# First keys loaded through GpSimd's own queue, and the second unit of a sketch-attention kernel divided by token

## The chip, the cores and the metric

The kernel runs on one core of one Trainium2 chip. A core has TensorE (matrix products, PE in the profile, with its weight loads as PEld), VectorE (DVE), ScalarE (ACT), GpSimd (POOL) and SyncE (SP), which here only issues transfers, and 16 DMA engines that all queues share. SBUF is the memory on the core; PSUM receives what TensorE computes. The metric is the time of one execution on the device in microseconds (us).

## What is computed

Two parts follow each other. The first is an attention in which the softmax is replaced by a product of two sketches, so that keys can be summed up first; the second is a mix of four experts with ReLU, weighted by gates.

```python
# q, k, v: (4 batches, 4 heads, 1088 tokens, 32); S1, S2: (8, 32)
def phi(x):
    a = np.einsum('rd,bhsd->bhsr', S1, x)
    b = np.einsum('rd,bhsd->bhsr', S2, x)
    return np.einsum('bhsi,bhsj->bhsij', a, b).reshape(*x.shape[:-1], r * r)   # 64 features
q_p, k_p = (phi(q), phi(k))
kv = np.einsum('bhsf,bhsd->bhfd', k_p, v)
z = np.sum(k_p, axis=2)
num = np.einsum('bhsf,bhfd->bhsd', q_p, kv)
den = np.einsum('bhsf,bhf->bhs', q_p, z)[..., None] + 1e-06
attn = num / den
x = attn.transpose(0, 2, 1, 3).reshape(4352, 128)
# experts: w1 (4, 128, 1024), w2 (4, 1024, 128), gates (4352, 4)
p = domain_probs / (domain_probs.sum(-1, keepdims=True) + 1e-09)
for e in range(4):
    h = np.maximum(x @ w1[e], 0.0)
    out += p[:, e:e + 1] * (h @ w2[e])
```

All of it is in float32. No query of a batch can be worked on before all keys of that batch are projected, multiplied and summed.

## The kernel before

The 4352 tokens are worked on in chunks by the experts (128, 448, 512 tokens and so on) and in units by the attention (128, 448 and 512 for the first batch). The attention leaves its result in `xT`, 128 partitions (4 heads x 32) by 4352 tokens, from which the experts' first products read. While the experts of one chunk run, the attention of later units is done in small pieces between their steps: each `yield` below ends a piece, and a rate that is reckoned from `needed` says how many pieces a step takes in.

The first loads, all on the sync queue but one half of S:

```python
    def load_rows(src, b, name, part=slice(0, S)):
        d = kn if name == "kn" else qn
        if b not in d:
            d[b] = lpool.tile([P, S], F32, tag=name, bufs=2, name=name)
        c, n = part.start, part.stop - part.start
        nc.sync.dma_start(d[b][:, part], bass.AP(src.tensor, src.offset + b * H * S * D + c, [[G * D, P], [1, n]]))
    ...
    for i, (eng, src) in enumerate(((nc.scalar, S1), (nc.sync, S2))):
        eng.dma_start(s_raw[R * i : R * i + R, :], src.bitcast(I32))
    ...
    load_rows(k, 0, "kn")                    # 128 rows of 1088 float32
    load_rows(q, 0, "qn", slice(0, P))       # 128 rows of 128 float32
    vn[0] = load_v(0)                        # four transfers of 128 KB, two of 16 KB
    warm = cpool.tile([P, 512], BF16, name="warm")
    nc.vector.memset(warm[:, :], 0.0)
    ...
    nc.sync.dma_start(dp..., domain_probs...)      # the gates' load
    ...                                            # ends, the rest of q, and the weights
    nc.gpsimd.memset(sk[:, :], 0.0)                # GpSimd's first instruction here
    ...                                            # memsets of sr, sq, kT, vx, own2, eps on GpSimd
    def keep_warm(n):
        for _ in range(n):
            wp = psum(ps_h, "h")
            nc.tensor.matmul(wp[:, :], warm[:, 0:P], warm[:, :], start=True, stop=True)

    keep_warm(10)
```

`keep_warm` multiplies zeros. VectorE then turns S1 and S2 into float32 (`s_T`), and ScalarE and GpSimd copy this into the block matrices `sk` (keys) and `sr` (first queries). What follows for the first batch and unit:

```python
    def start():
        for r in range(3):
            key_turn(b, r)                    # VectorE: kn -> kT
        qT = query_turn(b, 0, n)              # VectorE: qn -> qT
        ...
        key_project(b, 0, kf[0])              # TensorE: h <- sk, kT; ScalarE: fs
        key_project(b, 1, kf[1])
        next(value)                           # ScalarE: vn -> vx
        key_project(b, 2, kf[2])
        ...                                   # TensorE: o, num <- qT, sr
        ...                                   # VectorE and GpSimd: kp, the products of features
        ...                                   # TensorE: f <- vx, kp, the sum over the keys
        ...                                   # VectorE: qp, then kvz
        first = attend_first(b, 0, n, qp)
        ...
        key_blocks(b, kv)                     # VectorE: kvx
```

The division of the first two units goes by feature: numerator and denominator come with the tokens along the free axis, and the result goes straight into `xT`.

```python
    def attend_first(b, c, n, qp):
        nd = [psum(ps_n, "den"), psum(ps_n, "num")]
        ...                                   # for c == 0: 1e-6 added by a product with eps
        for i in range(2):
            for _ in range(2):
                on_side(lambda s: nd[i][half[s], 0:n], lambda s: kvzs[b][:, s, 1 - i, :],
                        lambda s: qp[s][:, 0:n], start=(i > 0 or c > 0), stop=True)
        yield
        nc.vector.transpose(dT[:, 0:n], nd[0][:, 0:n])
        yield
        ...                                   # for c > 0: add 1e-6
        nc.vector.reciprocal(rc[:, 0 : n // 32], column)
        nc.vector.transpose(_ap(rb, ...), _ap(rc, ...))       # spread over the 32 values of a head
        yield
        nc.vector.tensor_tensor(out=_ap(xT, 0, P, c, order), in0=nd[1]..., in1=rb..., op=ALU.mult)
        have[0] += n
        yield
```

All later units go by token: a tile of 128 tokens lies on the partitions, four heads of 32 numerators and one denominator along the free axis, and the quotient has to be turned back, through memory outside the core.

```python
    def attend(b, c, n, qp):
        nd = [psum(ps_n, "den"), psum(ps_n, "num")]
        for c0, m in unit_parts(b, c, n):
            T = blocks(m)                     # tiles on each side; (4, 3) for 448 tokens, (4, 4) for 512
            for t in range(T[0]):
                for p in range(2):
                    for _ in range(2):
                        ...
                        on_side(lambda s: nd[i][half[s], ...], lambda s: qp[p][:, at : at + HP],
                                lambda s: kvx[b][:, p, :], start=True, stop=True)   # 66 columns
        yield
        ...                                   # rc = 1 / (den + 1e-6), small
        yield
        ...                                   # xs = num * rc
        yield
        nc.vector.transpose(_ap(y, ...), _ap(xs, ...))
        ...                                   # sync: y -> xd (4 transfers), xd -> xT (1 transfer)
        have[0] += n
        yield

    def queries(b, c, n):
        ...                                   # qT, qc, qf, qb, qa, qp
        yield from (attend_first if b == 0 and c < START[2] else attend)(b, c, n, qp)
```

At step 13 of the first chunk GpSimd copies one column of `xT` (`behind`) and so waits for the second unit, before it starts its sums of weight blocks (`w2s`), which TensorE reads from the second chunk on.

Of the kernel before, what the change touches and what calls it, by code (L numbers as in the profile page):

```python
# [8 lines left out]
F32 = mybir.dt.float32  # L9
BF16 = mybir.dt.bfloat16  # L10
I32 = mybir.dt.int32
ALU = mybir.AluOpType
# [11 lines left out]
def kernel(  # L24
# [23 lines left out]
    nc = tc.nc  # L48

    P = 128  # L50
    HP = 64
    B, H, S, D = q.shape
# [31 lines left out]
        return pool.tile([P, 512], F32, tag=tag, name=tag)  # L84


    def load_rows(src, b, name, part=slice(0, S)):

        d = kn if name == "kn" else qn
        if b not in d:  # L90
            d[b] = lpool.tile([P, S], F32, tag=name, bufs=2, name=name)
        c, n = part.start, part.stop - part.start
        nc.sync.dma_start(d[b][:, part], bass.AP(src.tensor, src.offset + b * H * S * D + c, [[G * D, P], [1, n]]))

    def load_v(b):
        t = lpool.tile([P, H * NT * D], F32, tag="vn", name="vn")
# [15 lines left out]
    def load_batch(b):  # L112
        load_rows(k, b, "kn")
        vn[b] = load_v(b)
        load_rows(q, b, "qn")

    s_raw = cpool.tile([R2, 2 * D], I32, name="s_raw")
    for i, (eng, src) in enumerate(((nc.scalar, S1), (nc.sync, S2))):
        eng.dma_start(s_raw[R * i : R * i + R, :], src.bitcast(I32))  # L119
# [6 lines left out]
    def load_w2(e):  # L126
        nc.sync.dma_start(w2_sb[:, e], w2[e].rearrange("(f p) d -> p f d", p=P))

    load_rows(k, 0, "kn")
    load_rows(q, 0, "qn", slice(0, P))  # L130
    vn[0] = load_v(0)


    warm = cpool.tile([P, 512], BF16, name="warm")
# [5 lines left out]
    nc.sync.dma_start(  # L140
        dp.rearrange("p g e -> p (g e)"), bass.AP(domain_probs.tensor, domain_probs.offset, [[G * E, P], [1, G * E]])
    )

    ends = cpool.tile([P, 2, E], F32, name="ends")
    e_sum = cpool.tile([P, 2, 3], F32, name="e_sum")
# [31 lines left out]
    def keep_warm(n):  # L177

        for _ in range(n):
            wp = psum(ps_h, "h")  # L180
            nc.tensor.matmul(wp[:, :], warm[:, 0:P], warm[:, :], start=True, stop=True)  # L181

    keep_warm(10)


    turn = [0]
# [271 lines left out]
    def query_turn(b, c, n):  # L458


        qT = apool.tile([P, QW], F32, tag="qT", name="qT")
        for c0, m in unit_parts(b, c, n):
            src = c + c0
            if b == 0 and c < START[2]:
                todo = [([[1, m]], [[1, m]], 0, 0)]
            elif c0:
                todo = [([[32, 4], [1, 32]], [[1, 4], [4, 32]], 0, 0)]
            else:
                T = blocks(m)
                if T[0] == T[1]:  # L470
                    todo = [([[32 * T[0], 4], [32, T[0]], [1, 32]], [[32, 4], [P, T[0]], [1, 32]], 0, 0)]
                else:
                    todo = [
                        ([[32 * T[s], 2], [32, T[s]], [1, 32]], [[32, 2], [P, T[s]], [1, 32]], 64 * T[0] * s, HP * s)
                        for s in range(2)
                    ]
            for i, o, ci, co in todo:
                nc.vector.transpose(_ap(qT, 0, P, c0 + co, o), _ap(qn[b], 0, P, src + ci, i))
        return qT
# [12 lines left out]
    def attend_first(b, c, n, qp):  # L492


        nd = [psum(ps_n, "den"), psum(ps_n, "num")]
        if c == 0:
            for _ in range(2):
                on_side(
                    lambda s: nd[0][half[s], 0:n],
                    lambda s: _ap(vx, 0, P, D, [[0, HP]]),  # L500
                    lambda s: _ap(eps, 0, P, 0, [[0, n]]),
                    start=True,
                    stop=False,
                )
        for i in range(2):
            for _ in range(2):
                on_side(
                    lambda s: nd[i][half[s], 0:n],
                    lambda s: kvzs[b][:, s, 1 - i, :],
                    lambda s: qp[s][:, 0:n],  # L510
                    start=(i > 0 or c > 0),
                    stop=True,
                )
        yield
        dT = apool.tile([P, UNITS[0][1]], F32, tag="dT", name="dT")
        nc.vector.transpose(dT[:, 0:n], nd[0][:, 0:n])
        yield
        rc = apool.tile([P, QW // 32], F32, tag="rc", name="rc")
        column = _ap(dT, 0, P, 0, [[32, n // 32]])
        if c:  # L520
            nc.vector.tensor_scalar(
                out=rc[:, 0 : n // 32], in0=column, scalar1=1e-6, scalar2=1.0, op0=ALU.add, op1=ALU.mult
            )
            column = rc[:, 0 : n // 32]
        nc.vector.reciprocal(rc[:, 0 : n // 32], column)
        rb = apool.tile([P, UNITS[0][1]], F32, tag="rb", name="rb")
        nc.vector.transpose(
            _ap(rb, 0, P, 0, [[32, n // 32], [1, 32]]), _ap(rc, 0, P, 0, [[1, n // 32], [0, 32]])
        )
        yield  # L530

        order = [[1, 4], [4, 32]] if c == 0 else [[32, n // 32], [1, 32]]
        nc.vector.tensor_tensor(  # L533
            out=_ap(xT, 0, P, c, order),
            in0=nd[1][:, 0:n].rearrange("p (g j) -> p g j", j=32),
            in1=rb[:, 0:n].rearrange("p (g j) -> p g j", j=32),
            op=ALU.mult,
        )
        have[0] += n
        yield  # L540

    def attend(b, c, n, qp):

        nd = [psum(ps_n, "den"), psum(ps_n, "num")]
        W = H * (D + 1)
        tiles = 0
        laid = []
        for c0, m in unit_parts(b, c, n):  # L550
            T = blocks(m)
# [4 lines that stand above are left out]
                        at = c0 + P * t + (HP * turn[0] if t < T[turn[0]] else 0)  # L556
                        i, k = divmod(tiles + t, 3)
                        on_side(
                            lambda s: nd[i][half[s], W * k + W // 2 * p : W * k + W // 2 * (p + 1)],
                            lambda s: qp[p][:, at : at + HP],  # L560
                            lambda s: kvx[b][:, p, :],
                            start=True,
                            stop=True,
                        )
            laid.append((c0, T, tiles))
            tiles += T[0]
        yield
        banks = [(i, 3 * i, min(tiles, 3 * i + 3)) for i in range((tiles + 2) // 3)]
        rc = apool.tile([P, QW // 32], F32, tag="rc", name="rc")
        for i, t0, t1 in banks:  # L570
            nc.vector.tensor_scalar(
                out=rc[:, H * t0 : H * t1],
                in0=_ap(nd[i], 0, P, D, [[D + 1, H * (t1 - t0)]]),
                scalar1=1e-6, scalar2=1.0, op0=ALU.add, op1=ALU.mult,
            )
        nc.vector.reciprocal(rc[:, 0 : H * tiles], rc[:, 0 : H * tiles])
        yield
        xs = apool.tile([P, QW], F32, tag="qa", name="xs")
        for i, t0, t1 in banks:
            nc.vector.tensor_tensor(  # L580
                out=_ap(xs, 0, P, P * t0, [[D, H * (t1 - t0)], [1, D]]),
                in0=_ap(nd[i], 0, P, 0, [[D + 1, H * (t1 - t0)], [1, D]]),
                in1=_ap(rc, 0, P, H * t0, [[1, H * (t1 - t0)], [0, D]]),
                op=ALU.mult,
            )
        yield
        y = apool.tile([P, QW], F32, tag="y", name="y")
        for c0, T, t0 in laid:
            nc.vector.transpose(
                _ap(y, 0, P, P * t0, [[32, T[0]], [32 * T[0], H], [1, 32]]),  # L590
                _ap(xs, 0, P, P * t0, [[P, T[0]], [D, H], [1, D]]),
            )
            m = 64 * sum(T)
            base = xd.offset + P * (S * b + c + c0)
            for a in range(4):
                run = 32 * T[a // 2]
                nc.sync.dma_start(
                    bass.AP(
                        xd.tensor,
                        base + a // 2 * 64 * T[0] + a % 2 * run,  # L600
                        [[m, 32], [32 * m, H], [1, run]],
                    ),
                    _ap(y, 32 * a, 32, P * t0, [[32 * T[0], H], [1, run]]),
                )
            nc.sync.dma_start(
                xT[:, S * b + c + c0 : S * b + c + c0 + m],
                bass.AP(xd.tensor, base, [[m, P], [1, m]]),
# [5 lines that stand above are left out]
# [22 lines left out]
                yield  # L635
        yield
        yield
        yield from (attend_first if b == 0 and c < START[2] else attend)(b, c, n, qp)


    w2s = cpool.tile([P, E, FB // 2, 4, HP], F32, name="w2s")
# [277 lines left out]
    for b in range(B):  # L919
        count += 17 if b else 0  # L920
        for n in UNITS[b] if b else UNITS[0][1:]:
            count, columns = count + 19, columns + n
            for m in range(NC):
                if columns - n < START[m] + CHUNKS[m] <= columns:
                    needed[m] = count
# [70 lines left out]
```

## Time and profile before

| What | Value |
|---|---|
| median of three times | 490.6 us (490.52 to 491.0) |
| span of the profiled run | 488.9 us |
| TensorE busy | 482.5 us (99%) |
| VectorE, ScalarE, GpSimd busy | 322.1, 244.7, 226.6 us |
| share of TensorE in the chain that ended last | 96% |
| clock granted to TensorE | 1.00 throughout |
| memory traffic | 26.24 MB, mean 54 GB/s |

How to read it. Each line of the timeline is one instruction, or a run of like ones: its start and duration in us, the engine, the line in the kernel, the operation, what it writes and reads (destination <- source), the shape, and in brackets the idle time of its engine before it with what ended that. TensorE's float32 products show as two passes each, so 16 products are counted as 32. "SPq" is the issue of a transfer by the sync engine; the landing comes later. The chain of waits starts at the last instruction and is followed back: at each step to what released it, or to the instruction before it on its engine. A helper records most matrix products, so they all have its line; the tile names tell them apart: `h` holds key projections first and expert products later, `f` the key sums, `den` and `num` the second unit's products.

### The profile page before, as it was taken

Reading aid. Unit: us, or ns where it says so; the run is one execution under the profiler, and the core shown is the slowest. Engines: PE = TensorE matmul, PEld = TensorE weight load, DVE = VectorE, ACT = ScalarE, POOL = GpSimd, SP = SyncE. Lnnn points to the kernel's source line nnn. Section 1 sums busy time; section 2 is a strip of 40 time slices with the busy share of each in tenths; the row PEclk is TensorE's granted clock in tenths of the full one; section 3 lists DMA queues with packets and bytes.
Section 4 is the critical chain, followed back from the end, with each engine's and each line's share of the span. In section 5 each row is a group of like instructions: output and inputs, shape, how many; then the busy total and the mean of one; then the engine's idle time right before and its main releaser. Section 6 shows DMA issues by size and latency. Waiting matters only on the chain.

```text
span 488.9 us, 11239 instructions
## 1 busy us (share of the span) xinstructions
PE 482.5 (99%) x4498; PEld 358.8 (73%) x4498; DVE 322.1 (66%) x752; ACT 244.7 (50%) x488; POOL 226.6 (46%) x261
## 2 busy tenths in 40 slices
PE   8999999999999999999999999999999999999997
PEld 5877777677777777555777777777777777878996
DVE  5759685868676757768675665575575566655642
ACT  4344563455445634535455464445455455566651
POOL 6051473516345444334555353434555345555570
PEclk9999999999999999999999999999999999999999
DMA  7990230040102420041102200021101200120000
GB/s 209 289 297 10 87 96 1 11 127 1 34 1 87 117 71 1 0 119 24 34 1 87 50 0 3 0 87 24 33 1 56 50 0 1 50 50 2 16 1 18
DMA packets 37587, 26.24 MB, mean 54 GB/s; under 512 B 26016, under 2 KB 34592, under 8 KB 37024
## 3 DMA queue, kind: packets, MB, share of 16 engines
q1 hardware_dynamic: 37520, 25.53, 18.8%
q8 instruction: 35, 0.57, 0.5%
q14 instruction: 16, 0.13, 0.1%
q10 hardware_dynamic: 16, 0.00, 0.0%
HBM read 21.28 MB, written 4.24 MB: 52 GB/s over the span
## 4 chain that ended last, share of the span: by engine, by line
PE 96%; DVE 2%; DMA 1%; issue 0%; ACT 0%; SPq 0%; DVEq 0%
PE h L193 49%; PE o L193 40%; PE f L193 4%; PE den L193 2%; DMA kn<-in_k_dram 1%; DVE qp L485 1%; DVE hid L745 1%; PE num L193 0%; PE h L181 0%; DVE kT L319 0%; ACT hid L770 0%; DVE qa L631 0%; ACT sh L889 0%; SPq L119 0%; DVE xT L533 0%
## 5 line engine op out<-in xcount | busy, mean ns | idle before, releaser
L193 PE MATMUL h<-xT,w_sb 128*64 128x512 f32 (+4 forms) x1408 | 300.0, 495 | 0.3 <-DVE xT L533 0.3
L745 DVE SCALAR_TENSOR_TENSOR hid<-h,hid 128x256 f32<-128x256 f32 (+6 forms) x432 | 203.8, 472 | 143.4 <-ACT hid L770 134.6
L770 ACT ACTIVATE hid<-h 128x512 f32<-128x512 f32 (+3 forms) x288 | 158.3, 550 | 195.2 <-PE h L193 151.4
L193 PE MATMUL o<-hid,w2s 128*64 128x256 f32 (+3 forms) x1152 | 221.9, 355 | 0.0
L193 PE MATMUL o<-hid,w_sb 128*64 128x256 f32 (+3 forms) x864 | 183.5, 355 | 0.0
L193 PEld LDWEIGHTS h<-xT,w_sb 128*64 128x64 f32 x1408 | 143.3, 137 | 52.1 <-issue 10.9
L193 PEld LDWEIGHTS o<-hid,w2s 128*64 128x64 f32 x1152 | 132.6, 137 | 29.7 <-issue 0.2
L885 POOL TENSOR_TENSOR ev<-yz,sh 64x256 f32<-64x256 f32 (+3 forms) x72 | 47.9, 666 | 163.4 <-ACT sh L888 160.7
L193 PEld LDWEIGHTS o<-hid,w_sb 128*64 128x64 f32 x864 | 101.5, 137 | 26.1 <-issue 8.2
L873 POOL TENSOR_TENSOR yz<-ev 128x512 f32<-128x512 f32 (+3 forms) x36 | 42.2, 1173 | 61.1 <-ACT ev L876 61.0
L885 POOL TENSOR_TENSOR ct<-ev 128x512 f32<-128x512 f32 (+3 forms) x36 | 42.0, 1166 | 2.8
L485 DVE TENSOR_TENSOR qp<-qa,qb 64x384 f32<-64x384 f32 (+3 forms) x44 | 33.4, 758 | 1.0
L885 POOL TENSOR_TENSOR ct<-ct,gate 128x512 f32<-128x512 f32 (+3 forms) x27 | 32.3, 1196 | 2.1
L885 POOL TENSOR_TENSOR total<-total,ct 128x512 f32<-128x512 f32 (+3 forms) x27 | 32.0, 1187 | 2.1
L875 ACT COPY ev<-o 128x512 f32<-128x512 f32 (+3 forms) x36 | 19.4, 539 | 11.3 <-PE o L193 10.8
L193 PE MATMUL o<-w_sb,hid 128*64 128x128 f32 x256 | 21.6, 273 | 0.0
L876 ACT COPY ev<-o 128x512 f32<-128x512 f32 (+3 forms) x36 | 19.4, 540 | 2.4
L762 ACT ACTIVATE hid<-h 128x256 f32<-128x256 f32 x24 | 9.2, 385 | 20.9 <-PE h L193 20.3
L193 PEld LDWEIGHTS o<-w_sb,hid 128*64 128x64 f32 x256 | 17.8, 137 | 2.1 <-issue 1.9
L382 DVE TENSOR_TENSOR kp<-fs 128x256 f32<-128x256 f32 (+1 forms) x24 | 14.8, 619 | 0.1
L888 ACT COPY sh<-yz 64x256 f32<-64x256 f32 (+3 forms) x36 | 13.7, 379 | 1.6 <-POOL yz L873 0.8
L889 ACT COPY sh<-yz 64x256 f32<-64x256 f32 (+3 forms) x36 | 13.7, 380 | 0.9
(124 smaller groups left out, 231.7 us busy)
## 6 DMA issues: line engine op xcount, KB each, us to landing
w_sb<-in_moe_w_dram SPq DMA_DIRECT2D x8, 512.0 KB, 7.5
gate<-gates SPq DMA_DIRECT2D x4, 1024.0 KB, 4.9
kn<-in_k_dram SPq DMA_DIRECT2D x4, 544.0 KB, 4.9
vn<-in_v_dram SPq DMA_DIRECT2D x16, 128.0 KB, 4.3
gate<-gates SPq DMA_DIRECT2D x2, 896.0 KB, 4.7
qn<-in_q_dram SPq DMA_DIRECT2D x3, 544.0 KB, 5.8
xd<-y SPq DMA_DIRECT2D x26, 48.0 KB, 1.7
out_dram<-ob SPq DMA_DIRECT2D x16, 64.0 KB, 2.0
```

The lines of the kernel that those rows point to most:

```text
L193: nc.tensor.matmul(out(s), weights(s), moving(s), **flags)
L382: eng.tensor_tensor(out=_ap(kps[b], 0, P, 256 * t0 + P * p + 64 * x, [[256, n], [32, 2], [R, 4], [1, R]]), in0=_ap(src, 0, P, off + 4 * x, ...
L485: nc.vector.tensor_tensor(out=qp[p][64 * x : 64 * x + 64, 0:n], in0=qa[64 * p : 64 * p + 64, 0:n], in1=qb[64 * p : 64 * p + 64, 0:n], op=A ...
L745: nc.vector.scalar_tensor_tensor(out=out, in0=src, scalar=0.0, in1=in1, op0=ALU.max, op1=ALU.subtract)
L762: nc.scalar.activation(hd[:, 0 : 2 * n], hp[:, 0 : 2 * n], ACTF.Relu)
L770: nc.scalar.activation(hd[:, n * j : n * j + n], hp[:, 0:n], ACTF.Relu)
L873: add = lambda out, in0, in1, op=ALU.add: nc.gpsimd.tensor_tensor(out=out, in0=in0, in1=in1, op=op)
L875: nc.scalar.copy(_ap(ev, 0, P, 0, [[2 * w, 2], [1, w]]), _ap(a0, 0, P, 0, two))
L876: nc.scalar.copy(_ap(ev, 0, P, w, [[2 * w, 2], [1, w]]), _ap(a1, 0, P, 0, two))
L885: add = lambda out, in0, in1, op=ALU.add: nc.gpsimd.tensor_tensor(out=out, in0=in0, in1=in1, op=op)
L888: nc.scalar.copy(sh[HP:P, 0:w], yz[0:HP, 0, 0:w])
L889: nc.scalar.copy(sh[0:HP, 0:w], yz[HP:P, 1, 0:w])
```

## The change

It has two parts. The first batch's keys are issued by GpSimd, on its own queue and ahead of everything else, instead of being second in the sync queue; v goes one place back in the sync queue, behind the load of the gates; and two warming matmuls are left out. That is for an earlier start of the first projection.

The other part lets the second unit (448 tokens of batch 0) take the way of the later units: products by token against `kvx`, with 66 columns each, and a division by token. The way through outside memory is left out for it, as its result is wanted soon: after the transpose, 16 copies of 32 partitions, eight on ScalarE and eight on GpSimd, put `y` in place in `xT`. With the two more pieces this has, the count in `needed` goes from 19 to 21 for that unit. The first unit stays as it was, so what `attend_first` did for `c > 0` falls away.

```diff
--- before.py
+++ after.py
@@ -84,13 +84,13 @@
         return pool.tile([P, 512], F32, tag=tag, name=tag)
 
 
-    def load_rows(src, b, name, part=slice(0, S)):
+    def load_rows(src, b, name, part=slice(0, S), engine=nc.sync):
 
         d = kn if name == "kn" else qn
         if b not in d:
             d[b] = lpool.tile([P, S], F32, tag=name, bufs=2, name=name)
         c, n = part.start, part.stop - part.start
-        nc.sync.dma_start(d[b][:, part], bass.AP(src.tensor, src.offset + b * H * S * D + c, [[G * D, P], [1, n]]))
+        engine.dma_start(d[b][:, part], bass.AP(src.tensor, src.offset + b * H * S * D + c, [[G * D, P], [1, n]]))
 
     def load_v(b):
         t = lpool.tile([P, H * NT * D], F32, tag="vn", name="vn")
@@ -114,6 +114,7 @@
         vn[b] = load_v(b)
         load_rows(q, b, "qn")
 
+    load_rows(k, 0, "kn", engine=nc.gpsimd)
     s_raw = cpool.tile([R2, 2 * D], I32, name="s_raw")
     for i, (eng, src) in enumerate(((nc.scalar, S1), (nc.sync, S2))):
         eng.dma_start(s_raw[R * i : R * i + R, :], src.bitcast(I32))
@@ -126,9 +127,7 @@
     def load_w2(e):
         nc.sync.dma_start(w2_sb[:, e], w2[e].rearrange("(f p) d -> p f d", p=P))
 
-    load_rows(k, 0, "kn")
     load_rows(q, 0, "qn", slice(0, P))
-    vn[0] = load_v(0)
 
 
     warm = cpool.tile([P, 512], BF16, name="warm")
@@ -140,6 +139,7 @@
     nc.sync.dma_start(
         dp.rearrange("p g e -> p (g e)"), bass.AP(domain_probs.tensor, domain_probs.offset, [[G * E, P], [1, G * E]])
     )
+    vn[0] = load_v(0)
 
     ends = cpool.tile([P, 2, E], F32, name="ends")
     e_sum = cpool.tile([P, 2, 3], F32, name="e_sum")
@@ -180,7 +180,7 @@
             wp = psum(ps_h, "h")
             nc.tensor.matmul(wp[:, :], warm[:, 0:P], warm[:, :], start=True, stop=True)
 
-    keep_warm(10)
+    keep_warm(8)
 
 
     turn = [0]
@@ -461,7 +461,7 @@
         qT = apool.tile([P, QW], F32, tag="qT", name="qT")
         for c0, m in unit_parts(b, c, n):
             src = c + c0
-            if b == 0 and c < START[2]:
+            if b == c == 0:
                 todo = [([[1, m]], [[1, m]], 0, 0)]
             elif c0:
                 todo = [([[32, 4], [1, 32]], [[1, 4], [4, 32]], 0, 0)]
@@ -493,45 +493,37 @@
 
 
         nd = [psum(ps_n, "den"), psum(ps_n, "num")]
-        if c == 0:
-            for _ in range(2):
-                on_side(
-                    lambda s: nd[0][half[s], 0:n],
-                    lambda s: _ap(vx, 0, P, D, [[0, HP]]),
-                    lambda s: _ap(eps, 0, P, 0, [[0, n]]),
-                    start=True,
-                    stop=False,
-                )
+        for _ in range(2):
+            on_side(
+                lambda s: nd[0][half[s], 0:n],
+                lambda s: _ap(vx, 0, P, D, [[0, HP]]),
+                lambda s: _ap(eps, 0, P, 0, [[0, n]]),
+                start=True,
+                stop=False,
+            )
         for i in range(2):
             for _ in range(2):
                 on_side(
                     lambda s: nd[i][half[s], 0:n],
                     lambda s: kvzs[b][:, s, 1 - i, :],
                     lambda s: qp[s][:, 0:n],
-                    start=(i > 0 or c > 0),
+                    start=(i > 0),
                     stop=True,
                 )
         yield
-        dT = apool.tile([P, UNITS[0][1]], F32, tag="dT", name="dT")
+        dT = apool.tile([P, P], F32, tag="dT", name="dT")
         nc.vector.transpose(dT[:, 0:n], nd[0][:, 0:n])
         yield
         rc = apool.tile([P, QW // 32], F32, tag="rc", name="rc")
-        column = _ap(dT, 0, P, 0, [[32, n // 32]])
-        if c:
-            nc.vector.tensor_scalar(
-                out=rc[:, 0 : n // 32], in0=column, scalar1=1e-6, scalar2=1.0, op0=ALU.add, op1=ALU.mult
-            )
-            column = rc[:, 0 : n // 32]
-        nc.vector.reciprocal(rc[:, 0 : n // 32], column)
-        rb = apool.tile([P, UNITS[0][1]], F32, tag="rb", name="rb")
+        nc.vector.reciprocal(rc[:, 0 : n // 32], _ap(dT, 0, P, 0, [[32, n // 32]]))
+        rb = apool.tile([P, P], F32, tag="rb", name="rb")
         nc.vector.transpose(
             _ap(rb, 0, P, 0, [[32, n // 32], [1, 32]]), _ap(rc, 0, P, 0, [[1, n // 32], [0, 32]])
         )
         yield
 
-        order = [[1, 4], [4, 32]] if c == 0 else [[32, n // 32], [1, 32]]
         nc.vector.tensor_tensor(
-            out=_ap(xT, 0, P, c, order),
+            out=_ap(xT, 0, P, 0, [[1, 4], [4, 32]]),
             in0=nd[1][:, 0:n].rearrange("p (g j) -> p g j", j=32),
             in1=rb[:, 0:n].rearrange("p (g j) -> p g j", j=32),
             op=ALU.mult,
@@ -590,6 +583,16 @@
                 _ap(y, 0, P, P * t0, [[32, T[0]], [32 * T[0], H], [1, 32]]),
                 _ap(xs, 0, P, P * t0, [[P, T[0]], [D, H], [1, D]]),
             )
+            if b == 0 and c == P:
+                for x in range(2):
+                    yield
+                    for a in (x, x + 2):
+                        run = 32 * T[a // 2]
+                        for h in range(H):
+                            copy = nc.scalar.copy if h % 2 else nc.gpsimd.tensor_copy
+                            at = S * b + c + a // 2 * 64 * T[0] + a % 2 * run
+                            copy(xT[32 * h : 32 * h + 32, at : at + run], _ap(y, 32 * a, 32, 32 * T[0] * h, [[1, run]]))
+                continue
             m = 64 * sum(T)
             base = xd.offset + P * (S * b + c + c0)
             for a in range(4):
@@ -635,7 +638,7 @@
                 yield
         yield
         yield
-        yield from (attend_first if b == 0 and c < START[2] else attend)(b, c, n, qp)
+        yield from attend(b, c, n, qp)
 
 
     w2s = cpool.tile([P, E, FB // 2, 4, HP], F32, name="w2s")
@@ -919,7 +922,7 @@
     for b in range(B):
         count += 17 if b else 0
         for n in UNITS[b] if b else UNITS[0][1:]:
-            count, columns = count + 19, columns + n
+            count, columns = count + (19 if count else 21), columns + n
             for m in range(NC):
                 if columns - n < START[m] + CHUNKS[m] <= columns:
                     needed[m] = count
```

(One hunk that adds an empty line is left out.)

Compiled, the two kernels differ in nothing else: on each engine, all instructions after the first chunk's last steps are the same in the same order.

## The prediction, made before the changed kernel ran

> **What bounds the kernel now.** I read the page first, then the chain of waits from 0 to 30 us, then the timeline of the first 30 us, and last the stretches and the shapes of single groups.
>
> ```profile
> PE 482.5 (99%) x4498; PEld 358.8 (73%) x4498; DVE 322.1 (66%) x752; ACT 244.7 (50%) x488; POOL 226.6 (46%) x261
> ```
>
> This is the page's busy time. TensorE is busy 482.5 of 488.9 us, so the kernel is shortened only by less matmul work or by an earlier start of the dense part. The stretches show where TensorE isn't dense:
>
> ```profile
> 0.00:6.05 6.05, 4.26 (x10) 1.38 (x11) 2.77 (x17) 2.86 (x7) 3.81 (x23) 1.00 0.61 175
> 6.05:14.19 8.14, 7.58 (x184) 6.46 (x185) 5.94 (x23) 2.25 (x7) 3.91 (x13) 1.00 0.91 276
> 14.19:30.43 16.24, 16.24 (x256) 14.50 (x258) 11.25 (x30) 6.15 (x16) 3.91 (x7) 1.00 0.91 284
> ```
>
> The columns are stretch, length, then busy us and count of TensorE, its weight loads, VectorE, ScalarE and GpSimd. The first 6.05 us hold only the ten warming matmuls, which compute nothing. From 14.19 us on TensorE never rests. The chain of waits says what the first real matmul waits for:
>
> ```profile
> 0.74 0.41 SPq L119
> 1.15 0.06 issue
> 1.21 3.96 DMA kn<-in_k_dram
> 5.17 0.02 issue
> 5.20 0.72 DVE kT L319
> 5.92 0.14 issue
> 6.05 2.32 PE h L193 x72
> ...
> 23.46 0.75 PE den L193 x4
> 24.21 0.75 PE num L193 x4
> ```
>
> The load of k is issued second in the sync queue, at 1.21, lands at 5.17, is transposed, and the projections start at 6.05. The last two lines are the second unit's products, 1.50 us on the chain. The timeline gives the other ends that meet at the first projection:
>
> ```profile
> 3.80 0.23 DVE L232 STREAM_TRANSPOSE s_T<-s_hl 32x64 f32<-32x64 f32 x1
> 4.10 0.45 POOL L241 COPY sk<-s_T 32x32 f32<-32x32 f32 x2 [0.83 <-DVE s_T L232]
> 5.20 1.30 DVE L319 STREAM_TRANSPOSE kT<-kn 128x512 f32<-128x512 f32 x2 [1.16 <-DMA kn<-in_k_dram]
> 9.48 2.30 PE L193 MATMUL f<-vx,kp 128*64 128x66 f32 x72
> 26.18 0.62 DVE L533 TENSOR_TENSOR xT<-num,rb 128x448 f32<-128x448 f32 x1
> 30.43 1.70 PE L193 MATMUL h<-xT,w_sb 128*64 128x448 f32 x8
> ```
>
> VectorE is done with the sketch matrices at 4.03 and idles 1.16 us for k. GpSimd's sketch copies end at 4.55. The second unit's xT is ready at 26.80, the first matmul that reads it starts at 30.43.
>
> **What the Trainium skill says.** "DMA: Bandwidth & Descriptors", Specifications: a transfer issued by GpSimd has its first byte after about 1 us, one of the sync or scalar queue after about 0.6. Its section "Anatomy of one DMA — SWDGE (gpsimd) path" fits 2.0 us plus bytes over 436 GB/s. For k (128 rows of 4352 B, 557,056 B) that is 2.0 + 1.28 = 3.28 us. The trace has no GpSimd transfer; the sync one took 3.96 us, and before it data flowed slowly (109 GB/s from 2 to 3 us, 383 from 3 to 4). The same page, "Queues, rings and completion order", says that each DMA engine takes turns between queues by the packet. So k in a queue of its own need not wait behind S, but shares with q and v. No run here shows that yet. "SBUF — State Buffer", SBUF: two separate sides, warns that such a transfer's descriptors wait while VectorE holds the shared port. In the trace VectorE does only a fill of `warm` (0.87 to 1.14), one small fill, and then nothing until 2.38, so I expect little of it.
>
> **The change part by part.**
>
> (1) k's issue. GpSimd's first instruction after the start is now the transfer, so it starts near 0.74 (there the memset of sk starts) in place of 1.21. With the fit of the page it would land at 0.74 + 3.28 = 4.02. I add an estimated 0.5 us for sharing with q, the gates' load and v, since their small packets come between k's, and because the sync transfer needed more than the fit too. So landing at about 4.5, a gain of 5.17 - 4.5 = 0.67 us. Two floors stand close below: VectorE is free at 4.03 (gain at most 5.20 - 4.05 = 1.15), and the sketch copies on GpSimd. If writing the descriptors holds GpSimd for 1 us, as the 1 us of the page suggests, its memsets end at 4.27 instead of 3.27 and its sk copies at 4.7 instead of 4.55. With the first kT transpose at 4.52 to 5.24 and the 0.14 us of the chain, matmuls start at 5.38, so this floor doesn't bind. GpSimd's copies into sr, done at 5.75 before, end at about 6.0, and the query projections that read them start at 8.37 - 0.67 = 7.7.
>
> (2) Two warming matmuls fewer. They end near 5.45 now; at 0.43 us each, without two of them they end at 4.6. They would have held the start at 5.45 and cost 0.07 us against my 5.38; otherwise this brings nothing by itself.
>
> (3) v behind the gates' load. In the sync queue k (0.37 us of issue) goes and the gates' load (0.35) comes before v: v is issued at 2.05 instead of 2.09. v's copies on ScalarE begin at 8.44 now, directly behind other ScalarE work; moved up by 0.67 they begin at 7.8. The DMA share falls to 0.27 from 7 to 8 us, so v has landed in time.
>
> From 6.05 to 14.19 everything hangs on the first projection, so the whole 0.67 us goes through.
>
> (4) The second unit on TensorE. Removed: 4 products of 448 columns, which the trace counts as 8 passes, 2 x 0.75 = 1.50 us of the chain. Added: 4 tiles x 2 halves x 2 sides = 16 products of 66 columns, 32 passes. The chain has 72 passes of this shape in 2.12 us (the key sums), 0.0294 each, so 32 x 0.0294 = 0.94 us. Saved: 0.56 us, in a stretch in which TensorE is 100% busy, so all of it counts.
>
> (5) The same on VectorE. Removed: 0.65 + 0.17 + 0.24 + 0.65 + 0.62 = 2.33 us. Added, from the third unit, which has the same 4 tiles: 0.16 + 0.15 + 0.25 + 0.56 + 0.28 + 0.70 = 2.10 us; the query transpose is cut in two, some 0.05 us. Nothing of this is on the chain: VectorE is 11.25 of 16.24 us busy there.
>
> (6) The 16 copies. On ScalarE a 32x32 copy takes 0.216 us and 64x256 0.379, so 32x128 and 32x96 are some 0.25: four at a time, 1.0 us, twice. On GpSimd 32x32 takes 0.20 and 32x192 0.334, so some 0.28, eight in a row, 2.2 us. Timing: the products start at 23.46 - 0.67 = 22.8 and end at 23.7; 2.1 us of VectorE later, y is there at about 25.8. ScalarE's thirteenth rectifier ends at 27.19 - 1.23 = 25.96, so its copies run 26.0 to 27.0 and, after one rectifier of 0.38, 27.4 to 28.4. GpSimd's run 25.8 to 28.1. The matmul that reads xT would start at 30.43 - 1.23 = 29.20, 0.8 us later. The rectifiers in between come up to 1.1 us late, but their readers on TensorE are two steps (1.75 us) behind. So nothing stalls. GpSimd's weight sums begin at about 28.4 instead of 27.01; the first four (0.7 each) end at 31.2, and TensorE first reads them at 35.81 - 1.23 = 34.6.
>
> After this, all engines have the same instructions in the same order. I expect a pure shift up to the end.
>
> Sum: 0.67 + 0.56 = 1.23 us; 490.6 - 1.23 = 489.4 us.
>
> **The rivals.** (a) GpSimd's transfer is slower than the sync one: descriptor writing by software, or a first use of that code, or v's packets between k's. Then k lands at 5.4 or later, the first eight warming matmuls leave TensorE idle, and only part (4) is left, or less: 490.0 to 490.5, with a landing after 5.8 even a loss. For it: the page gives GpSimd's path the longer first byte, and 0.47 us of earlier issue is about all it gets in exchange. Against it: the sync queue's own transfer shows 0.68 us over the page's fit, and someone took two warming matmuls out, which suits an earlier k. (b) k lands by 4.1 and VectorE's sketch chain becomes the bound: a gain of 1.15 + 0.56 = 1.7, 488.9 us. GpSimd's delayed copies into sk would then be the nearer bound, so I give it less. (c) The copies are late: y or the last GpSimd copy arrives after 29.2 and TensorE waits for it. With the 0.8 us of slack above, copies of 0.4 us each on GpSimd would be needed; each 0.1 us over costs 0.8 us at the end of the row of eight. Then the 0.56 us are gone: 489.9 or more. (d) v comes late for the key sums, because k in its own queue takes bandwidth from it: then part of (1) is given back at the key sums, 489.7.
>
> **Range and chances.** Part (4) is arithmetic on measured passes: 0.4 to 0.6 us. Part (1) is the open one: from -0.3 (slow descriptors) to 1.1 us (the floor). The times before spread over 0.5 us. Together: 488.5 to 490.6 in 8 of 10 cases, most likely 489.4. Two per cent are 9.8 us, more than the whole startup could give back, and no part can cost so much: within 2% has 0.98, faster 0.01, slower 0.01.
>
> **What would show it.** In the changed profile, k's landing near 4.5, VectorE's idle time before the first kT transpose down from 1.16 to about 0.5 us, and the first projection at 5.4. The first reader of xT (128 columns) at 13.5 instead of 14.19. The second unit's products as 32 passes in about 0.95 us. The first matmul of 448 columns at 29.2 with no idle time behind a ScalarE or GpSimd copy. The shift at 30 us equal to the shift at the end. Wrong would be: a GpSimd transfer that takes over 4.4 us to land, TensorE waiting at the key sums for v's copies, or a wait of the 448-column step for GpSimd.

## The result, and the profile after

| | before | changed |
|---|---|---|
| median time | 490.63 us | 492.52 us |
| lowest to highest (6 runs each) | 490.44 to 491.0 | 491.38 to 494.03 |
| ratio of the times, 95% interval | | 1.0042 [1.0022, 1.0063] |
| profiled run: time, span | 490.67, 488.9 us | 494.03, 491.2 us |

The changed kernel is 1.9 us slower, and its times scatter over 2.7 us where those of before keep within 0.6. The first of these lines is the busy time on the page of the changed kernel, the second is one of its DMA queues (packets, MB, share of 16 engines), here GpSimd's new one:

```profile
PE 482.8 (98%) x4520; PEld 361.3 (74%) x4520; DVE 322.9 (66%) x754; ACT 246.7 (50%) x496; POOL 229.2 (47%) x270
...
q0 software_dynamic: 144, 0.56, 0.3%
```

TensorE's busy time is no guide here: it is 0.3 us above that of before although the second unit needs less work. The chain of waits of the changed kernel (start, duration, what) shows where the time went:

```profile
0.64 0.61 issue
1.25 5.11 DMA kn<-in_k_dram
6.36 0.02 issue
6.38 0.72 DVE kT L319
7.10 0.14 issue
7.24 3.15 PE h L193 x72
10.39 1.65 PE o L193 x16
...
26.26 0.70 PE den L193 x24
26.96 0.23 PE num L193 x8
```

Set beside the chain of before, three rows account for the startup. The keys land at 6.36 instead of 5.17: 1.19 us. The 72 passes of the key projections take 3.15 us instead of 2.32: 0.83. The 16 of the query projections take 1.65 instead of 0.88: 0.77. That makes 2.79 us, and the experts' first product starts at 16.99 instead of 14.19, 2.80 later. The last two rows are the second unit: 0.93 us instead of 1.50. By the first 448-column step the delay is 32.66 - 30.43 = 2.23 us, so 0.57 came back, and the span ends 2.3 us later. Everything after the first chunk is a pure shift.

The same 72 passes take longer because each of them does. The stretches of the changed kernel (stretch, length, busy us and count of TensorE, its weight loads, VectorE, ScalarE, GpSimd, then the granted clock, DMA share, GB/s):

```profile
7.00:8.00 1.00, 0.76 (x26) 0.79 (x28) 1.00 (x4) 0.00 (x0) 0.00 (x0) 1.00 0.77 107
8.00:9.00 1.00, 1.00 (x33) 1.00 (x30) 0.17 (x2) 0.37 (x1) 0.05 (x1) 0.72 0.65 135
9.00:10.00 1.00, 1.00 (x25) 1.00 (x23) 0.59 (x2) 0.00 (x0) 1.00 (x2) 0.50 0.97 346
5.02:8.43 3.41, 1.19 (x41) 1.22 (x43) 1.62 (x4) 1.16 (x5) 1.28 (x5) 1.00 0.91 188
8.43:11.85 3.42, 3.42 (x56) 3.42 (x53) 1.99 (x7) 2.22 (x7) 1.97 (x4) 0.50 0.93 308
11.85:15.26 3.41, 3.16 (x91) 2.92 (x89) 1.94 (x8) 0.02 (x1) 1.93 (x10) 1.00 1.05 344
```

TensorE rested from 4.79, where the eight warming matmuls end, to 7.24. At 8.43, after 1.19 us of work, its granted clock fell to a half, until 11.85. "Busy" stays at 1.00 through it. In before one us holds up to 42 such passes.

The last three lines are cut where the trace's own record of the clock changes: full from 5.02 to 8.43, half from 8.43 to 11.85, then full again. Ahead of its first entry the record is empty, and the clock column prints 1.00 there. In before the first entry is at 5.14, so the clock of 1.00 "throughout" is known only from there on; its ten warming matmuls start 427 ns apart, while the last five of the thirteen in `e3_warm13` below start 216 ns apart.

The last view is the changed kernel's timeline, with the lines that the prediction had named:

```profile
1.25 0.75 POOL L93 DMA_DIRECT2D kn<-in_k_dram  x1 [0.80 <-POOLq L983]
2.38 0.89 DVE L205 TENSOR_SCALAR s_f<-s_raw 16x32 int32<-16x32 int32 x1 [1.18 <-DMA s_raw<-in_S_dram]
28.51 0.71 DVE L582 STREAM_TRANSPOSE y<-xs 128x512 f32<-128x512 f32 x1
29.28 2.47 POOL L594 COPY xT<-y 32x128 f32<-32x128 f32 x8 [10.24 <-DVE y L582]
31.05 1.16 ACT L594 COPY xT<-y 32x128 f32<-32x128 f32 x4
32.66 1.70 PE L193 MATMUL h<-xT,w_sb 128*64 128x448 f32 x8
```

GpSimd's transfer starts at 1.25, not at 0.74: the head start over the sync queue (1.21 before) is gone before it begins. The copies end at 31.75 (GpSimd) and 32.21 (ScalarE), the step that reads them starts at 32.66 with nothing waited for.

### The profile page after: what moved, and what is told of

Its sections match the earlier page's. It is cut to its first block, busy times and chain, and to the rows that moved or that the text cites. A ratio compares the mean times of both kernels' runs of the same rounds, so it can differ in the third digit from the quotient of the medians.

```text
span 491.2 us, 11304 instructions
## 1 busy us (share of the span) xinstructions
PE 482.8 (98%) x4520; PEld 361.3 (74%) x4520; DVE 322.9 (66%) x754; ACT 246.7 (50%) x496; POOL 229.2 (47%) x270
## 4 chain that ended last, share of the span: by engine, by line
PE 96%; DVE 2%; DMA 1%; issue 1%; ACT 0%; DVEq 0%; POOLq 0%
PE h L193 49%; PE o L193 40%; PE f L193 4%; PE den L193 2%; DMA kn<-in_k_dram 1%; DVE qp L485 1%; DVE hid L748 1%; PE num L193 0%; PE h L181 0%; DVE kT L319 0%; ACT hid L773 0%; DVE qa L634 0%; ACT sh L892 0%; DVE end L812 0%; DVE kvz L405 0%
## 5 line engine op out<-in xcount | busy, mean ns | idle before, releaser
L485 DVE TENSOR_TENSOR qp<-qa,qb 64x384 f32<-64x384 f32 (+3 forms) x44 | 32.4, 736 | 1.0
L382 DVE TENSOR_TENSOR kp<-fs 128x256 f32<-128x256 f32 (+1 forms) x24 | 16.3, 684 | 0.1
L193 PEld LDWEIGHTS den<-kvx,qp 128*64 128x64 f32 x264 | 12.3, 137 | 3.7 <-issue 1.1
L891 ACT COPY sh<-yz 64x256 f32<-64x256 f32 (+3 forms) x36 | 13.6, 379 | 1.6 <-POOL yz L876 0.8
```

Of the source, the lines that this page charges most:

```text
L193: nc.tensor.matmul(out(s), weights(s), moving(s), **flags)
L382: eng.tensor_tensor(out=_ap(kps[b], 0, P, 256 * t0 + P * p + 64 * x, [[256, n], [32, 2], [R, 4], [1, R]]), in0=_ap(src, 0, P, off + 4 * x, ...
L485: nc.vector.tensor_tensor(out=qp[p][64 * x : 64 * x + 64, 0:n], in0=qa[64 * p : 64 * p + 64, 0:n], in1=qb[64 * p : 64 * p + 64, 0:n], op=A ...
L891: nc.scalar.copy(sh[HP:P, 0:w], yz[0:HP, 0, 0:w])
```

## The experiments

My theory after the comparison: both losses are in the first part. GpSimd's transfer is late, and the rest that this gives TensorE, lengthened by two missing warming matmuls, costs it the clock. The rival was that the second part takes something too, or that the clock falls for another reason. Every run was set beside runs of the kernel before on the same chip; their medians were 490.78 us (for `e1` to `e4`), 490.77 (`e5`, `e6`, `e7`, `e9`), 490.61 (`e8`, `e10`) and 490.59 (`e11`, `e12`). Differences given in us are between medians.

**Each part alone.** The first run takes only the first hunks into the kernel before, the second only the later ones:

```diff
# e1_keys: the kernel before, with
+    load_rows(k, 0, "kn", engine=nc.gpsimd)
-    load_rows(k, 0, "kn")
-    vn[0] = load_v(0)          # now behind the gates' load
-    keep_warm(10)
+    keep_warm(8)
# e2_token: the changed kernel, with these lines put back
```

> The first part of the change alone (keys issued by GpSimd, v behind the gates' load, eight warming matmuls), on the kernel before. Theory: all of the loss sits here. GpSimd's transfer lands some 5.1 us after its issue at 1.25, TensorE then rests 2.4 us, its clock falls to a half for some 3 us, and the experts' first product starts at about 17.0 us instead of 14.2: up to 2.8 us lost where the clock falls, 1.2 where it doesn't; a median of 491.8 to 493.4 us. Rival: the loss comes from the second unit's copies or their waits; then this run is within 0.5 us of the kernel before, 490.6.

> The second part alone (second unit divided by token with the copies), with the loads and the ten warming matmuls of the kernel before. Theory: it is worth the 0.56 us reckoned from the passes, 490.1 us, and the first 448-column step starts at 29.9 us instead of 30.4. Rival (copies late): 490.6 us or more, with an idle TensorE ahead of the 448-column step.

The first part alone: 493.28 us (491.61 to 494.44), ratio 1.0049 [1.0036, 1.0063]. The second alone: 490.36 us against 490.78, ratio 0.9992 [0.9984, 1.0]; run again as `e10_token`, 490.39 against 490.61, ratio 0.9998 [0.9992, 1.0005].

> The second part alone once more, beside the run above on the same chip: 0.4 to 0.6 us below the kernel before.

So the loss is all in the first part. The second is at most a small gain of time, 0.42 and 0.22 us; the second figure is less than I had expected, and its interval includes 1. The gain is clearer in the spans: their medians are 488.2 against 489.0 us and 488.4 against 488.8. In the profile of `e2_token` the first 448-column step starts at 29.86 instead of 30.43, exactly the 0.57 us of the passes, and the span is 488.3 instead of 488.9. That less of it shows in the time has a cause that I did not find: in before the time is 1.73 to 1.84 us longer than the span in every run, in these two up to 3.2 us, and in the changed kernel's profiled run 2.83.

By luck the keys landed early in the profiled run of `e2_token`, which shows what earlier keys were worth in this one run. Its timeline:

```profile
4.76 1.30 DVE L319 STREAM_TRANSPOSE kT<-kn 128x512 f32<-128x512 f32 x2 [0.65 <-DMA kn<-in_k_dram]
5.62 2.73 PE L193 MATMUL h<-sk,kT 128*64 128x64 f32 x72
14.19 1.06 PE L193 MATMUL h<-xT,w_sb 128*64 128x128 f32 x15 [0.32 <-PE h L181]
```

The projections start 0.43 us earlier than in before and take 0.4 us longer, as their first passes last over 300 ns instead of 222; the experts' first product starts at 14.19, as before. TensorE's clock had not come up yet: its record begins at 6.56 here, against 5.14 in before.

**Is it the rest that costs the clock?**

```diff
# e3_warm13: the changed kernel
-    keep_warm(8)
+    keep_warm(13)
# e5_warm8 and e6_warm6: the kernel before
-    keep_warm(10)
+    keep_warm(8)               # 6 in the second
# e12_keys13: e1_keys
-    keep_warm(8)
+    keep_warm(13)
```

> The changed kernel with 13 warming matmuls instead of 8, so that TensorE is busy until about 6.8 us, when the keys are nearly there. Theory (the clock falls because TensorE rested): the granted clock stays at 1.00 from 7 to 14 us, the key projections take 2.3 us instead of 3.15 and the query projections 0.9 instead of 1.65; the loss shrinks by 1.6 us in the runs where the clock fell, to about 491.2 us (490.6 + 1.2 for the later keys - 0.6 for the second unit), with a narrower spread. Rival (the clock falls by itself, whatever TensorE does): the clock is at 0.5 again between 8 and 12 us and the median stays near 492.5.

491.22 us (490.85 to 491.71), ratio 1.0008 [1.0, 1.0017]. With the longer warming, the spread is gone and 1.3 us of the 1.9 too. I had expected TensorE to work until 6.8; the last five matmuls ran at the full clock, so it worked until 5.69 and still rested 1.27 us. A stretch and the first projection:

```profile
8.00:9.00 1.00, 1.00 (x42) 1.00 (x39) 0.45 (x2) 0.37 (x1) 0.34 (x1) 1.00 0.97 173
6.96 2.32 PE L193 MATMUL h<-sk,kT 128*64 128x64 f32 x72 [1.27 <-DVE kT L319]
```

42 passes in one us at a clock of 1.00, where the changed kernel has 33 and then 25. The key projections take 2.32 us again and the query projections 0.88.

> The kernel before with eight warming matmuls instead of ten, nothing else changed: TensorE rests from about 4.8 to 6.05 us, 1.3 us instead of 0.6. Theory (a long rest lets the clock fall, and the changed kernel's 2.4 us are long): 1.3 us are mostly too short, so the clock stays at 1.00 and the median is within 0.3 us of 490.7. Rival (the two matmuls themselves matter, as the clock rises only after a fixed amount of work): the first projections run at the slow rate (over 300 ns a pass instead of 222) and the median is 0.5 to 1.5 us higher.

> The kernel before with six warming matmuls: TensorE rests from about 3.9 to 6.05 us, 2.1 us, near the changed kernel's 2.45, while the keys still come by the sync queue at 5.2. Theory: the fall of the clock comes from the rest alone, so it shows here too in many runs: 0.5 of the clock for up to 3 us within 6 to 12 us, key projections of 3 us or more, a median of 491.2 to 492.5 us and a wide spread. Rival (the fall needs GpSimd's transfer or the later keys): clock 1.00 throughout and 490.7 us.

Eight: 492.02 us, ratio 1.0017 [1.0007, 1.0026]; six: 491.8 us, ratio 1.0014 [1.0002, 1.0026]. Both fall into two groups with nothing between. With eight, five of 13 runs lie at 490.4 to 490.8 and eight at 492.0 to 492.7; with six, six lie at 490.4 to 490.7 and seven at 491.8 to 493.1. My expectation for eight was wrong: I had thought the shorter rest harmless, yet two matmuls that compute nothing, taken out of the kernel before, cost 1.25 us in the median and 0.8 in the mean. The profiled run with eight belongs to the lower group, the one with six to the upper. The first projection with eight, then two stretches with six:

```profile
5.86 2.32 PE L193 MATMUL h<-sk,kT 128*64 128x64 f32 x72 [1.17 <-POOL sr L248]
6.00:7.00 1.00, 1.00 (x20) 1.00 (x22) 0.72 (x3) 0.00 (x0) 0.00 (x0) 1.00 1.04 172
7.00:8.00 1.00, 1.00 (x24) 1.00 (x23) 0.00 (x0) 0.03 (x1) 0.00 (x0) 1.00 0.24 30
```

20 and 24 passes in one us where before has up to 42, so TensorE is at half its rate, while the clock column says 1.00; the record of the clock begins at 9.18 in this trace. So there are two ways to lose the clock. In the changed kernel's profile it was up and fell after the rest; here it had not come up yet. The column shows only the first; counting passes shows both. My expectation for six named the right median for the wrong reason, a fall.

Nor is it the length of the rest alone: `e3_warm13` and `e5_warm8` rest about as long (1.27 and 1.17 us), but the one has 4.49 us of warming before that and no slow group of runs, the other has 3.49 and is slower in eight of 13 runs.

The Trainium skill, "TensorE: Matmul & The Clock Gate", Part 1, says that the array starts at half its clock and gets the whole after some 3.4 us of work, judged by windows that run freely, whatever the kernel does. I had not drawn on it for the prediction. The traces agree with its core. The half clock of the changed kernel lasts 3.41 us, and so does that of `e1_keys` (7.97 to 11.38). In every trace the 3.41 us ahead of the first entry hold at least 2.77 us of work (`e9_hold`), 3.41 in before; in `e6_warm6` the 3.41 us ahead of those held 1.58, and the clock had not risen. After it had risen, it fell where the next 3.41 us held 1.19 us of work (the changed kernel) or 1.15 (`e1_keys`), and stayed where they held 1.47 (`e8_first` below), 1.99 (`e12_keys13`) or 2.15 (`e3_warm13`). On these figures it is the work within such a window that decides, and where its edges fall differs from run to run, which fits a loss that comes in some runs only. For the way down the page names an idle window; here windows with over a us of work were followed by half the clock. With ten warming matmuls all but one of the 106 runs of before lie below 491.4 us.

> The first part alone with thirteen warming matmuls: what the later keys cost without the clock. Theory: the landing 0.9 to 1.2 us later shows in full and nothing else, 491.6 to 492.0 us with a narrow spread. Rival (the later keys are partly hidden behind other waits of the startup, and the clock makes nearly all of the loss): 491.2 us or less.

491.98 us (491.57 to 492.55), ratio 1.0029 [1.0018, 1.004]. So the later keys alone cost 1.39 us; the keys landed at 6.26, 1.09 after those of before. With eight warming matmuls it was 2.50 us, so the clock adds 1.1. GpSimd's keys with ten warming matmuls were not run, so how much of this the two missing ones cost, and how much the longer rest would have cost with all ten, stays open. The nearest is `e8_first` below: ten warming matmuls, a first projection at 7.74, times that scatter over 3.3 us, and one run of six with a mean clock of 0.995.

**Why are the keys late?**

```diff
# e4_scalar: the changed kernel, k on ScalarE's queue behind S1, ten warming matmuls
-    load_rows(k, 0, "kn", engine=nc.gpsimd)
+    load_rows(k, 0, "kn", engine=nc.scalar)      # below the loop that loads S1 and S2
-    keep_warm(8)
+    keep_warm(10)
# e9_hold: the changed kernel; everything on the sync queue behind the gates' load
# is issued only after ScalarE has written four elements of v's tile
+    nc.scalar.copy(hold[0:1, 0:1], sr[64:65, 0, 0, 0:1])      # and for rows 32, 64, 96
+    vn[0] = load_v(0, hold)
# e7_late: e2_token, with the keys of batches 1 to 3
-        load_rows(k, b, "kn")
+        load_rows(k, b, "kn", engine=nc.gpsimd)
```

> The changed kernel with the keys on ScalarE's queue, behind its half of S, and ten warming matmuls: still a queue of its own beside q, the gates and v, but not GpSimd's. Theory (GpSimd's own way to start a transfer is what is slow): issued at about 1.3, landed by 5.0 to 5.4, so the first projection starts near 6.1 and the time is near 490.0 us. Rival (sharing with v's transfers slows the keys, whichever queue they are in): landing after 6.0 us and 491 us or more.

> The changed kernel with v and all later loads of the sync queue held back until ScalarE's sketch copies are done (four one-element copies into v's tile make them wait), so that after 3 us nothing shares the DMA engines with the keys. v, the rest of q and the weights come later for it, so its time will be worse and isn't asked for. Theory A (most of the 5.1 us is GpSimd's own start): the keys land at 5.8 us or later, and still 4.5 us or more after the issue. Theory B (sharing with v's packets): they land at 5.3 us or earlier, 4.1 us or less after the issue.

> The second part alone, with the keys of batches 1 to 3 issued by GpSimd (the first batch's by sync as before). They are off the path that sets the end, so only the time from issue to landing is asked for; sync's took 4.9 us in the median over its four. Theory (GpSimd's way is slow every time): 4.5 us or more where nothing else is loading. Rival (only the first use is slow): 3.3 us or less in the later batches.

On ScalarE's queue the keys were issued at 1.35 and landed at 5.15, 3.81 us later, beside the same v transfers; the time was 490.86 us, ratio 1.0006 [0.9996, 1.0015]. So a queue of its own isn't what makes them late. It brought nothing either, though this run has the second part too and I had expected 490.0; the chain of that run shows one more floor of the startup:

```profile
7.50 6.63 DMA w_sb<-in_moe_w_dram
14.14 0.14 issue
```

The first expert's first weights land at 14.14 there, and at 13.6 in before. Keys that came 0.67 us earlier would have brought its first product there to 14.19 - 0.67 = 13.52, and so met this wait next.

With v held back, GpSimd's transfer landed at 5.72, 4.5 us after its issue, between what the two theories asked for. In the other profiles it was 4.8 to 5.1 us: sharing with the loads that were held back explains roughly half (0.35 to 0.64 us, from one profile with them held back) of what it loses against the sync queue's 3.96. The packets show the parts. In before the first packet of k moves 0.99 us after the issue, the last one ends 2.39 us later, and the landing follows 0.58 us after that. In the changed kernel these are 1.50, 2.82 and 0.79 us; with v held back 1.49, 2.65 and 0.33. So the late first packet, 0.5 us, has nothing to do with v. In the changed kernel the queue had moved only 0.10 of its 0.56 MB by 3.6 us, in before the sync queue had moved 0.28 MB by 3.5. But GpSimd's queue isn't slow every time: in the middle of the kernel (`e7_late`), with little else loading, the same 544 KB took 4.0 and 3.9 us from issue to landing, where sync's took 5.1 and 4.7; the one at 16.2 us, while the weights loaded, took 7.5, and sync's at 25.2 in before took 8.2. Neither expectation of `e7_late` held. What is special about the first one, a first use, the first instructions being fetched or the memory being busy, stays open. `e9_hold` took 494.03 us and `e7_late` 491.88, one run each, which is read for nothing else.

**A better version?**

```diff
# e8_first: e2_token, with k first on the sync queue and
-    for i, (eng, src) in enumerate(((nc.scalar, S1), (nc.sync, S2))):
+    for i, (eng, src) in enumerate(((nc.scalar, S1), (nc.scalar, S2))):
+    load_w1(0)                                   # ahead of the rest of q
# e11_token12: e2_token
-    keep_warm(10)
+    keep_warm(12)
```

> Drawn from the runs so far: the second part, with the keys first in the sync queue (both halves of S on ScalarE's), ten warming matmuls, and the first expert's first weights ahead of the rest of q. Theory: the keys land at about 4.7 us and the first weights well before 13 us, but TensorE's clock rises only between 5.4 and 6.7 us, so little of the 0.47 us comes through: 489.8 to 490.3 us. Rival (the start follows the keys all the way): 0.4 us below the second part alone, 489.7 or less, with the experts' first product at 13.7 us.

> The best version the runs so far point to: the second part alone with twelve warming matmuls, so that TensorE works without a rest until the keys are turned. Theory: as the second part alone, with no run in which the clock is late; 490.0 to 490.4 us, at most 0.1 us lost where the warming matmuls end after the keys are there. Rival: the two more matmuls hold the first projection up, 490.8 us or more.

`e8_first`: 493.08 us, ratio 1.0049 [1.0032, 1.0067]. My expectation was wrong: it only exchanged waits. The second half of S, 2 KB, now landed after the keys, at 5.24, and the first projection started at 7.74.

```profile
5.34 0.17 DVE L207 TENSOR_SCALAR s_f<-s_raw 16x32 int32<-16x32 int32 x1 [4.14 <-DMA s_raw<-in_S_dram]
```

`e11_token12`, the second part with the loads of before and twelve warming matmuls: 490.12 us (489.75 to 490.72) against 490.59, ratio 0.999 [0.9982, 0.9998]. It is the only version whose interval stays below 1. Its spans are no shorter than those of `e10_token` (medians 488.3 and 488.4 us); what it has ahead is that the time stays 1.7 to 1.9 us above the span in every run, and why the second part with ten warming matmuls does not is the same open question as above. So it isn't shown that the two more matmuls are what makes it faster.

## Why the prediction was wrong

The prediction was 489.4 us, 488.5 to 490.6; the time is 492.52. It had the sign of the second part right and that of the first part wrong.

**Step (1), the keys' landing, failed.** "So landing at about 4.5, a gain of 5.17 - 4.5 = 0.67 us" was built on an issue at 0.74 and on an estimate, the skill's fit of 3.28 us plus 0.5. Measured: issue at 1.25, 5.11 us to land (4.8 to 5.1 in the other profiles of this transfer), landing at 6.36. The term has the wrong sign: a loss of 1.19 us in the profile, 1.39 us in the time with the clock held (`e12_keys13`). Its own sign of being wrong, over 4.4 us to land, came true. Rival (a) had named it, a landing "after 5.8 even a loss", and I gave it too little; the range's lower end of -0.3 us for this part was too narrow. The head start of 0.47 us was taken from where a memset starts; in the same place the transfer started 0.51 us later. The sync transfer's 3.96 us, the only measured start of a load of this shape here, should have carried more weight than a fit.

**Step (2), the warming matmuls, failed.** "Otherwise this brings nothing by itself" took them for filler. They bring TensorE's clock up in time: two fewer cost 1.25 us in the median on the kernel before (`e5_warm8`), and eight instead of thirteen 1.1 to 1.3 us on top of the later keys (`e1_keys` against `e12_keys13`, the changed kernel against `e3_warm13`). The prediction never asked what the matmuls are for, though it saw the 0.6 us of rest after them.

**"The whole 0.67 us goes through" fell as well.** It never came to the test in the changed kernel, but the profiled run of `e2_token` had keys 0.4 us early and nothing came of it, because TensorE ran at half rate until 6.56; and `e4_scalar` shows the weights' landing as the next wait.

**Step (3)** was right: v was issued at 2.10, and nothing waited for it. **Step (4)** was right: 0.94 us predicted, 0.93 measured, 0.57 us back at the 448-column step. **Step (5)** was right: from the first division to the end of y 2.2 us, and not on the chain. **Step (6)** was right in its verdict with sizes too small: GpSimd's eight copies took 2.47 us instead of 2.2 and ScalarE's fours 1.17 instead of 1.0, so the slack was 0.45 us, not 0.8. Rivals (b), (c) and (d) did not occur. The pure shift after the first chunk was right.

In sum: +1.4 (keys), +1.1 to 1.3 (clock), -0.2 to -0.5 (second unit) make 2.0 to 2.5 us, beside 1.9 measured.

## What to carry to other kernels

Before matmuls on zeros are cut, or the work behind them moved, ask how long TensorE will rest and whether it will have worked long enough for its clock; then look at several runs, because such a loss comes in some runs and not in others. Count passes per us, not busy time, where a stretch seems slow. Don't take an engine's first free moment for the moment its transfer starts (0.74 and 1.25 us here): take issue and landing from a transfer of that engine, and when one wait of a startup is to go, list which others end within a microsecond of it (here the sketch matrices, the clock and the first weights).

## What the runs showed that I had not expected

GpSimd's memsets, moved back by the transfer, now ran beside VectorE's first operations on S: three small ones took 0.89, 0.82 and 0.75 us instead of 0.17 and ended together near 3.3 us, while GpSimd's memsets ran one after another, so `s_T` was ready at 4.70 instead of 4.03. The copies into `sk` ended at 5.22, where the prediction had 4.7. That was hidden behind the keys, but it was the next floor: in `e9_hold`, where the keys landed at 5.72, the sketch copies into `sr` ended at 6.47, at the same time as the first transpose of the keys. The Trainium skill, "SBUF — State Buffer", SBUF: two separate sides, describes a port that the two engines share and lock for a whole instruction; the timeline fits that, and no run here separates it.
